# An attention and feed-forward kernel on one core: w_out loaded in four pieces, the fold in quarters, one part of q turned by a transfer, and all queues listed anew

## The chip, the core and the metric

The kernel runs on one core of a Trainium2 chip. A core has five engines that each follow their own queue of instructions: TensorE (PE, matmuls; its weight loads are listed as PEld), VectorE (DVE), ScalarE (ACT), GpSimd (POOL) and SyncE (SP, which only issues transfers here). 16 DMA engines move data; they are fed by POOL (loads that convert f32 to f16 on the way, and some others) and by SP (all other loads, the stores and the turning transfers). The metric is the device time of one execution in microseconds. A profiled execution gives a span, from its first to its last instruction, and there is some time around the span.

## The reference

Linear attention over 8 batches, 8 heads, 576 tokens and 64 channels per head, and then a gated product with four weight matrices, all in f32 at the boundary:

```python
q_s = softmax(q, axis=-1)          # over the 64 channels of a token
k_s = softmax(k, axis=2)           # over the 576 tokens of a batch
kv  = einsum('bhsd,bhse->bhde', k_s, v)
x   = einsum('bhsd,bhde->bhse', q_s, kv)     # -> 4608 x 512
a, b = x @ w1, x @ w2              # 512 -> 1024
h = a * b @ w3                     # 1024 -> 1024
out = h @ w_out                    # 1024 -> 512
```

Both softmaxes subtract a maximum first and add 1e-9 to the sum.

## The kernel before

Since nothing stands between w3 and w_out, the kernel first multiplies them: the **fold** W3O = w3 @ w_out, in eight row blocks ft of 128. After that each token costs two products with w1 and w2 and one with W3O.

All work is cut into named steps. A plan holds for each step its engine, what it needs and what buffers it takes. The class Plan emits the steps in the order of a written list, ORDER (lines 80 to 150), and each engine then runs its own steps in that order, one after another: a step that waits holds up all later steps of its engine. PICKS names the engine of the steps that can run on more than one. The tile framework puts in the waits for data. [...]

The names, for batch b (or chunk c, which is the first 512 tokens of the batch of the same number; chunk 8 is made of the last 64 tokens of every batch):

- loads: k.b, q.b, v.b, w1.i, w2.i (four column pieces each), w3.i (six row pieces) and wo.i (w_out). The first two parts of q go out on SP, the list LOADS on POOL, the rest on SP. A load on POOL waits for the landing of the one eight places ahead on POOL. q.0 and q.1 are loaded in two parts, q.b.0 (tokens blocks 0 to 3) and q.b.1 (blocks 4 to 8).
- fold: w3t.ft turns a block of w3 by eight TensorE transposes (line 415), w3T.ft moves it out of PSUM, pf.ft.h multiplies part h of it with part h of w_out (line 427), W3O.ft scales and stores the result (line 431). There are WOS parts, each of N_FT / WOS = 4 matmuls of 128x512 before the change.
- k: kmx (maximum), cb (the maximum brought to all partitions), ksub (subtract, line 490), kexp, and vc (v to f16, batches 2 and up). kv.b (lines 515 and 524) is the product with v, kv2.b divides by the sums.
- q: qmx, qsub (548), qexp (556), qsm (sum, 561), qeps, qrc (reciprocal), qn (multiply, 580), each in two parts p. Then q has to be turned so that channels lie on partitions. This is done in one of two ways: qt and qT are TensorE transposes (line 595) and an eviction from PSUM, qt.b.0 for part 0 and qt.b.8 and qt.b.16 for the blocks of part 1; or qd.b.p, one turning transfer on SP (line 603), for which DMAT[b][p] is set. Before the change batches 0 and 1 use TensorE and batches 2 to 7 the transfer.
- xm.b.h and xt.b (line 621) are the products with kv, for 512 tokens and for the last 64; xs and xts are their evictions.
- chunk: up.1 and up.0 (line 735) are the products with w2 and w1, bs evicts the first, ab (750) multiplies the two on DVE, down.c.tb (757) is the product with W3O, os its eviction and st.c.tb its store, as two transfers on SP.

Chunk 1 is worked in two halves of 256 tokens, so that xm.1.0 needs only part 0 of q of batch 1, and xm.1.1 and xt.1 need part 1.

PSUM is shared by rings: four buffers for up (and w3t), two for down and the fold, two for all of attention. The evicted outputs have four buffers in SBUF, so os waits for the store four places earlier. A load of batch b into a buffer of batch b - 2 waits for the exponentials of that batch (k.4 for kexp.2, q.4 for qexp.2).

FILL names two places where TensorE is given products of zeros: 17 at the start, and 16 ahead of pf.4.0.

Of the kernel before, what the change touches and what calls it, by code (L numbers as in the profile page):

```python
# [80 lines left out]
q.0.1 q.0.0 w3.4 k.0 wo.0 wo.1 ident w3.3 w3.0 qmx.0.1 w3.1 q.1.0 qsub.0.1 qexp.0.1 qmx.0.0 w3t.5
v.0 w3t.4 qsm.0.1 w3T.4 qsub.0.0 qeps.0.1 w3.5 qexp.0.0 kmx.0.0 w3T.5 w3.2 pf.4.0 qrc.0.1 cb.0
qn.0.1 pf.5.0 pf.4.1 qsm.0.0 k.1 qt.0.8 W3O.4 w2.0 w3t.3 qeps.0.0 ksub.0.1 pf.5.1 w3T.3 w1.0
qt.0.16 w3t.0 qrc.0.0 qT.0.8 qn.0.0 pf.3.0 kexp.0.1 pf.3.1 w3T.0 ksub.0.0 w3t.1 W3O.5 qt.0.0
w3T.1 W3O.3 pf.0.0 qmx.1.0 pf.1.0 kexp.0.0 qT.0.0 pf.0.1 qT.0.16 qsub.1.0 k.2 kv.0 w2.1 W3O.0
qexp.1.0 pf.1.1 w1.1 kv2.0 w3t.7 w2.2 qsm.1.0 w3t.6 w3T.7 xm.0.1 w1.2 w3t.2 xs.0.1.0 w3T.6 pf.7.0
W3O.1 xs.0.1.1 pf.7.1 qeps.1.0 pf.6.0 w3T.2 W3O.7 v.1 kmx.1.0 xm.0.0 pf.6.1 xs.0.0.1 xs.0.0.0
pf.2.0 w2.3 up.1.0.0.0 w1.3 qrc.1.0 up.0.0.0.0 cb.1 bs.0.0.0 qn.1.0 up.1.0.0.1 up.0.0.0.1
bs.0.0.1 ab.0.0.0 ksub.1.0 qt.1.0 kmx.2.0 pf.2.1 qT.1.0 up.1.0.0.2 W3O.2 xt.0 bs.0.0.2 q.1.1
ab.0.0.1 up.0.0.0.2 kexp.1.0 ksub.1.1 up.1.0.0.3 ab.0.0.2 xts.0.0 kmx.2.1 up.0.0.0.3 bs.0.0.3  # L90
up.1.0.0.4 up.0.0.0.4 bs.0.0.4 ab.0.0.3 kexp.1.1 up.1.0.0.5 xts.0.1 cb.2 up.0.0.0.5 W3O.6
bs.0.0.5 kv.1 q.2 ab.0.0.4 ksub.2.0 up.1.0.0.6 v.2 kv2.1 k.3 up.0.0.0.6 bs.0.0.6 ab.0.0.5 xm.1.0
ab.0.0.6 up.1.0.0.7 xs.1.0.1 ksub.2.1 xs.1.0.0 up.0.0.0.7 bs.0.0.7 qmx.1.1 kexp.2.0 up.1.1.0.0
up.0.1.0.0 ab.0.0.7 qsub.1.1 kexp.2.1 up.1.1.0.1 qmx.2.1 bs.1.0.0 up.0.1.0.1 bs.1.0.1 ab.1.0.0
down.0.0 qsub.2.1 qexp.1.1 qmx.2.0 vc.2.0 ab.1.0.1 q.3 up.1.1.0.2 v.3 qsm.1.1 vc.2.1 up.0.1.0.2
k.4 qexp.2.1 up.1.1.0.3 qsub.2.0 os.0.0 qsm.2.1 up.0.1.0.3 qeps.1.1 bs.1.0.2 kv.2 qrc.1.1
qexp.2.0 ab.1.0.2 down.0.1 qn.1.1 kv2.2 bs.1.0.3 q.4 st.0.0 ab.1.0.3 down.0.2 os.0.1 qmx.3.1
st.0.1 qt.1.8 os.0.2 qeps.2.1 qrc.2.1 qt.1.16 qsub.3.1 down.0.3 qsm.2.0 qT.1.8 st.0.2 qT.1.16
qmx.3.0 xm.1.1 down.1.0 xs.1.1.0 qn.2.1 kmx.3.1 xs.1.1.1 up.1.1.1.0 vc.3.0 qeps.2.0 up.0.1.1.0
qexp.3.1 qd.2.1 qrc.2.0 kmx.3.0 qn.2.0 xt.1 up.1.1.1.1 os.0.3 up.0.1.1.1 bs.1.1.0 xts.1.0  # L100
qsub.3.0 qd.2.0 up.1.1.1.2 xts.1.1 bs.1.1.1 qsm.3.1 ab.1.1.0 os.1.0 down.1.1 bs.1.1.2 ab.1.1.1
st.1.0 up.0.1.1.2 os.1.1 qmx.4.1 up.1.1.1.3 v.4 st.1.1 ab.1.1.2 up.0.1.1.3 bs.1.1.3 qeps.3.1
st.0.3 xm.2.0 vc.3.1 ab.1.1.3 down.1.2 xs.2.0.1 cb.3 xs.2.0.0 qsub.4.1 qexp.3.0 xm.2.1 down.1.3
xs.2.1.0 qrc.3.1 xs.2.1.1 qsm.3.0 ksub.3.1 qexp.4.1 up.1.2.0.0 up.0.2.0.0 qeps.3.0 bs.2.0.0
vc.4.0 qrc.3.0 up.1.2.0.1 ab.2.0.0 ksub.3.0 xt.2 kmx.4.0 bs.2.0.1 up.0.2.0.1 up.1.2.0.2
up.0.2.0.2 bs.2.0.2 qn.3.0 xts.2.1 ab.2.0.1 kexp.3.0 up.1.2.0.3 ab.2.0.2 up.0.2.0.3 qmx.4.0
bs.2.0.3 qn.3.1 kexp.3.1 up.1.2.0.4 os.1.2 up.0.2.0.4 bs.2.0.4 xts.2.0 ab.2.0.3 up.1.2.0.5 qd.3.1
qsm.4.1 qeps.4.1 up.0.2.0.5 bs.2.0.5 qd.3.0 kv.3 qrc.4.1 qsub.4.0 ab.2.0.4 up.1.2.0.6 k.5 kv2.3
up.0.2.0.6 q.5 bs.2.0.6 st.1.2 ab.2.0.5 qn.4.1 up.1.2.0.7 ab.2.0.6 up.0.2.0.7 bs.2.0.7 xm.3.1
ab.2.0.7 down.2.0 xs.3.1.1 qd.4.1 kmx.4.1 xs.3.1.0 os.1.3 v.5 xm.3.0 down.2.1 xs.3.0.1 cb.4  # L110
xs.3.0.0 os.2.0 up.1.3.0.0 st.2.0 xt.3 kmx.5.0 up.0.3.0.0 xts.3.1 ksub.4.0 st.1.3 bs.3.0.0
up.1.3.0.1 os.2.1 up.0.3.0.1 st.2.1 bs.3.0.1 qmx.5.0 xts.3.0 down.2.2 qexp.4.0 ksub.4.1 qmx.5.1
kexp.4.0 down.2.3 ab.3.0.0 qsub.5.1 ab.3.0.1 up.1.3.0.2 qsm.4.0 up.0.3.0.2 bs.3.0.2 qeps.4.0
qsub.5.0 up.1.3.0.3 kexp.4.1 ab.3.0.2 up.0.3.0.3 qrc.4.0 bs.3.0.3 up.1.3.0.4 qn.4.0 ab.3.0.3
qexp.5.0 os.2.2 up.0.3.0.4 bs.3.0.4 qsm.5.0 up.1.3.0.5 qexp.5.1 vc.4.1 qd.4.0 up.0.3.0.5 ab.3.0.4
bs.3.0.5 qsm.5.1 up.1.3.0.6 st.2.2 kv.4 bs.3.0.6 k.6 ab.3.0.5 up.0.3.0.6 qeps.5.0 q.6 qrc.5.0 v.6
qeps.5.1 up.1.3.0.7 kv2.4 qn.5.0 up.0.3.0.7 bs.3.0.7 ab.3.0.6 os.2.3 xm.4.1 ab.3.0.7 down.3.0
xs.4.1.1 qrc.5.1 xs.4.1.0 kmx.5.1 qn.5.1 xm.4.0 down.3.1 xs.4.0.1 xs.4.0.0 cb.5 qd.5.1 up.1.4.0.0
up.0.4.0.0 bs.4.0.0 os.3.0 up.1.4.0.1 ksub.5.1 ab.4.0.0 xt.4 qmx.6.1 bs.4.0.1 up.0.4.0.1 down.3.2
ksub.5.0 ab.4.0.1 kexp.5.1 up.1.4.0.2 vc.5.0 up.0.4.0.2 bs.4.0.2 vc.5.1 kexp.5.0 up.1.4.0.3  # L120
ab.4.0.2 qsub.6.1 up.0.4.0.3 xts.4.0 bs.4.0.3 k.7 os.3.2 qd.5.0 up.1.4.0.4 xts.4.1 ab.4.0.3 kv.5
bs.4.0.4 st.2.3 up.0.4.0.4 os.3.1 kv2.5 vc.6.0 st.3.0 up.1.4.0.5 ab.4.0.4 up.0.4.0.5 qexp.6.1
qmx.6.0 q.7 st.3.1 up.1.4.0.6 bs.4.0.5 qsub.6.0 up.0.4.0.6 v.7 bs.4.0.6 ab.4.0.5 st.3.2
up.1.4.0.7 ab.4.0.6 vc.6.1 qsm.6.1 xm.5.0 qexp.6.0 up.0.4.0.7 xs.5.0.0 down.3.3 qeps.6.1 bs.4.0.7
ab.4.0.7 qrc.6.1 xs.5.0.1 down.4.0 qsm.6.0 qn.6.1 os.3.3 st.3.3 kmx.6.0 xm.5.1 os.4.0 down.4.1
xs.5.1.0 st.4.0 xs.5.1.1 qeps.6.0 qrc.6.0 qd.6.1 xt.5 kmx.6.1 os.4.1 up.1.5.0.0 qn.6.0 xts.5.0
xts.5.1 up.0.5.0.0 st.4.1 vc.7.0 up.1.5.0.1 cb.6 qd.6.0 vc.7.1 up.0.5.0.1 down.4.2 bs.5.0.0
ksub.6.0 ab.5.0.0 up.1.5.0.2 os.4.2 bs.5.0.1 up.0.5.0.2 st.4.2 bs.5.0.2 ab.5.0.1 up.1.5.0.3
ab.5.0.2 ksub.6.1 kexp.6.0 bs.5.0.3 up.0.5.0.3 ab.5.0.3 up.1.5.0.4 qmx.7.1 up.0.5.0.4 bs.5.0.4
kexp.6.1 up.1.5.0.5 ab.5.0.4 qsub.7.1 up.0.5.0.5 bs.5.0.5 qmx.7.0 up.1.5.0.6 ab.5.0.5 kv.6  # L130
qsub.7.0 bs.5.0.6 qexp.7.1 up.0.5.0.6 kv2.6 up.1.5.0.7 ab.5.0.6 up.0.5.0.7 bs.5.0.7 qsm.7.1
# [744 lines left out]
```

## Time and profile before

| | us |
|---|---|
| median of 3 runs (243.4 to 244.03) | 243.53 |
| the profiled execution, its own time | 243.27 |
| its span | 241.5 |
| TensorE busy | 234.5 (97% of the span) |
| DVE busy | 170.8 |
| POOL busy | 124.0 |
| ACT busy | 123.4 |
| mean granted TensorE clock | 1.000 |
| moved by DMA | 45.66 MB, mean 189 GB/s |

The profile's page gives busy time per engine and the span in 40 slices. A timeline line gives the start, the length, the engine, the line of the kernel, the operation with output and inputs, and in brackets the idle time ahead of it with what ended it. The length of several matmuls in one line is from the start of the first to the modelled end of the last; the start of the next step is the better measure of when TensorE came free. The chain that ended last is followed back from the end of the span: 88% of it is TensorE.

### The profile page before, as it was taken

How to read it: one execution, taken by the hardware profiler on the slowest of the kernel's cores; microseconds unless marked ns; L12 is line 12 of the kernel's file. 1: busy time of each engine (PE TensorE's matmuls, PEld its weight loads, DVE VectorE, ACT ScalarE, POOL GpSimd, SP SyncE). 2: the span in 40 equal slices, each digit the busy share in tenths (PEclk: the TensorE clock that was granted, in tenths of full speed). 3: DMA queues.
4: the chain of work that ended last, by engine and by line, in shares of the span. 5: the costliest groups of instructions: out<-in, count | busy, mean ns of one | idle time of the engine just before them, and what ended most of it. 6: DMA issues, size and time to landing. Idle time of an engine off the chain costs nothing.

```text
span 241.5 us, 4827 instructions
## 1 busy us (share of the span) xinstructions
PE 234.5 (97%) x1917; PEld 114.6 (47%) x1917; DVE 170.8 (71%) x293; ACT 123.4 (51%) x194; POOL 124.0 (51%) x79
## 2 busy tenths in 40 slices
PE   7889999999999999999999999999999999999994
...
PEclk9999999999999999999999999999999999999999
DMA  6999999999999808992897999701750215000343
GB/s 209 310 209 250 305 302 200 249 370 356 399 388 160 274 1 114 380 341 83 206 400 124 248 401 281 153 0 35 165 76 3 49 38 133 0 0 0 88 132 130
DMA packets 37894, 45.66 MB, mean 189 GB/s; under 512 B 15984, under 2 KB 22384, under 8 KB 37872
## 3 DMA queue, kind: packets, MB, share of 16 engines
...
q14 instruction: 7, 0.06, 0.1%
...
## 4 chain that ended last, share of the span: by engine, by line
PE 88%; DMA 7%; POOL 2%; issue 1%; ACT 0%; POOLq 0%
PE pab L735 52%; PE po L757 23%; DMA v<-in_v_dram 7%; PE po L772 3%; PE po L427 3%; PE pkv L515 2%; PE xm L621 2%; POOL w L377 1%; PE w3t L415 1%; PE xt L621 1%; PE pkv L524 1%; POOL wosb L377 0%; PE qtp L595 0%; POOL q L377 0%; POOL k L377 0%
## 5 line engine op out<-in xcount | busy, mean ns | idle before, releaser
L750 DVE TENSOR_TENSOR ab<-pab,bsb 128x512 f16<-128x512 f32 x72 | 48.8, 684 | 28.4 <-PE pab L735 24.8
L735 PE MATMUL pab<-x,w1sb 128*128 128x512 f16 (+1 forms) x288 | 65.9, 356 | 0.0
L735 PE MATMUL pab<-x,w2sb 128*128 128x512 f16 (+1 forms) x288 | 65.8, 356 | 0.0
L298 ACT CAST bsb<-pab 128x512 f16<-128x512 f32 x59 | 34.6, 586 | 52.0 <-PE pab L735 51.7
L757 PE MATMUL po<-W3O,ab 128*128 128x512 f16 x256 | 59.5, 380 | 0.0
L490 POOL TENSOR_TENSOR k<-k,cb 128x1152 f32<-128x1152 f32 x15 | 39.2, 2629 | 20.3 <-DVE cb L486 19.1
L735 PEld LDWEIGHTS <-w2sb 128*128 128x128 f16 x320 | 30.7, 98 | 30.6 <-issue 0.2
L735 PEld LDWEIGHTS <-w1sb 128*128 128x128 f16 x320 | 30.6, 98 | 29.6 <-issue 0.2
L580 POOL TENSOR_TENSOR en<-eq,qr 128x1280 f16<-128x1280 f16 (+1 forms) x15 | 32.1, 2141 | 15.3 <-ACT x L302 6.3
L757 PEld LDWEIGHTS <-ab 128*128 128x128 f16 x256 | 24.0, 98 | 29.2 <-issue 2.7
L548 POOL TENSOR_TENSOR q<-q,qm 128x1024 f32<-128x1024 f32 (+1 forms) x14 | 29.7, 2126 | 8.6 <-DVE qm L543 6.3
L298 ACT COPY osb<-po 128x512 f32<-128x512 f32 (+1 forms) x29 | 16.6, 572 | 28.5 <-PE po L757 22.6
L459 DVE TENSOR_REDUCE km<-k 128x128 f32<-128x1152 f32 x12 | 25.4, 2115 | 0.0
L543 DVE TENSOR_REDUCE qm<-q 128x20 f32<-128x1280 f32 (+1 forms) x16 | 21.4, 1344 | 4.1 <-DMA q<-in_q_dram 4.1
L302 ACT ACTIVATE x<-xm 128x512 f16<-128x512 f32 x30 | 16.5, 595 | 10.0 <-PE xm L621 9.8
L561 DVE TENSOR_REDUCE qr<-eq 128x20 f32<-128x1280 f16 (+1 forms) x16 | 21.3, 1330 | 0.4 <-ACT eq L556 0.4
L556 ACT ACTIVATE eq<-q 128x1280 f16<-128x1280 f32 (+1 forms) x16 | 18.6, 1165 | 5.6 <-POOL q L548 2.9
L498 ACT ACTIVATE ek<-k 128x1152 f16<-128x1152 f32 x16 | 18.5, 1164 | 2.5 <-POOL k L490 2.5
L298 DVE CAST bsb<-pab 128x512 f16<-128x512 f32 x13 | 9.0, 690 | 13.4 <-PE pab L735 13.3
L427 PE MATMUL po<-wosb,w3T 128*128 128x512 f16 x64 | 15.3, 379 | 1.2 <-DMA wosb<-in_moe_w_out_dram 1.2
L325 PE MATMUL po<-zero 128*128 128x512 f16 x33 | 10.0, 470 | 1.6 <-DVE zero L320 1.6
L427 PEld LDWEIGHTS <-w3T 128*128 128x128 f16 x64 | 5.8, 98 | 7.8 <-ACT w3T L298 1.2
...
## 6 DMA issues: line engine op xcount, KB each, us to landing
...
```

Source lines behind the costliest of these rows:

```text
L298: return [(nc.scalar.copy if eng == "ACT" else engine[eng].tensor_copy)(out=out, in_=in_)]
L427: nc.tensor.matmul(st["pf", ft], lhsT=st["w3T", ft][:, gt, :], rhs=wosb[:, gt, :], start=(gt == 0), stop=(gt == N_FT - 1))
L459: dve.tensor_reduce(out=st["km", b][:, two(hp), :], in_=kb[:, two(hp), :, :].rearrange("p h j d -> p h d j"), axis=AX.X, op=ALU.max)
L490: return [engine[eng].tensor_tensor(out=kb[:, two(hp), :, :], in0=kb[:, two(hp), :, :], in1=st["cb", b][:, two(hp), None, :].broadcast_to( ...
L543: dve.tensor_reduce(out=st["qm", b][:, :, j], in_=qb[:, :, j, :], axis=AX.X, op=ALU.max)
L548: return [engine[eng].tensor_tensor(out=qb[:, :, j, :], in0=qb[:, :, j, :], in1=st["qm", b][:, :, j, None].broadcast_to([P, HH, n, D]), op ...
L556: nc.scalar.activation(out=st["eq", b, p], in_=qb[:, :, j, :], func=AF.Exp)
L561: dve.tensor_reduce(out=st["qr", b][:, :, slice(*PARTS[p])], in_=st["eq", b, p], axis=AX.X, op=ALU.add)
L580: return [engine[eng].tensor_tensor(out=st["en", b][:, j, :, :].rearrange("p j h d -> p h j d"), in0=st["eq", b, p], in1=st["qr", b][:, :, ...
L735: nc.tensor.matmul(st["p", one, c, sub, u][:, a * (t1 - t0):(a + 1) * (t1 - t0)], lhsT=w[:, ct, fb * P:(fb + 1) * P], rhs=x()[:, ct, t0:t1 ...
L750: dve.tensor_tensor(out=st["ab", c][:, nf * u:nf * u + nf, t0:t1], in0=cut(st["p", 0, c, sub, u]), in1=cut(st["bsb", c, sub, u]), op=ALU.mult)
L757: nc.tensor.matmul(st["po", c, tb], lhsT=st["ab", c][:, ft, tb * P:(tb + 1) * P], rhs=W3O[:, ft, :], start=(ft == 0), stop=(ft == N_FT - 1))
```

## The change

1. WOS goes from 2 to 4: w_out is loaded in four pieces of 256 KB (as f16), in the order 0, 2, 1, 3, and each pf step has two matmuls.
2. DMATP = [(1, 1)]: part 1 of q of batch 1 is turned by the transfer qd.1.1 on SP. The steps qt.1.8, qt.1.16, qT.1.8 and qT.1.16 go.
3. ORDER, LOADS, PICKS, FILL and LINKED are new. In the list the differences reach to about batch 5. FILL now has 12 zero products ahead of qt.0.8 and none ahead of pf.4.0.

Core of the diff, with the loads and with the parts of the list that the prediction speaks of:

```diff
-LINKED = 191
+LINKED = 212
 FILL = {
-    "begin": 17, "pf.4.0": 16,
+    "begin": 17, "qt.0.8": 12,
 }
 LOADS = [
-    ("w3", 4), ("k", 0), ("wo", 0), ("wo", 1), ("w3", 3), ("w3", 0), ("w3", 1), ("q", 1, 0),
-    ("v", 0), ("w3", 5), ("w3", 2), ("k", 1), ("w2", 0), ("w1", 0), ("k", 2), ("w2", 1),
-    ("w1", 1), ("w2", 2), ("w1", 2), ("v", 1), ("w2", 3), ("w1", 3), ("q", 1, 1),
+    ("w3", 4), ("k", 0), ("wo", 0), ("wo", 2), ("wo", 1), ("wo", 3), ("w3", 3), ("w3", 0),
+    ("w3", 1), ("q", 1, 0), ("w3", 5), ("v", 0), ("w3", 2), ("k", 1), ("w1", 0), ("w2", 0),
+    ("k", 2), ("w2", 1), ("w1", 1), ("w2", 2), ("w1", 2), ("v", 1), ("w2", 3), ("w1", 3),
+    ("q", 1, 1),
 ]
-    WOS = 2
+    WOS = 4
-    DMATP = []
+    DMATP = [(1, 1)]
     DMAT = [[b > DMATS or (b, p) in DMATP for p in range(2)] for b in range(B)]
```

The list, sorted by engine (TensorE to the first up, POOL to the end of the loads, SP from its third load to the transposes of batch 2):

```
PE before:  w3t.5 w3t.4 pf.4.0 pf.5.0 pf.4.1 qt.0.8 w3t.3 pf.5.1 qt.0.16 w3t.0 pf.3.0 pf.3.1 w3t.1
            qt.0.0 pf.0.0 pf.1.0 pf.0.1 kv.0 pf.1.1 w3t.7 w3t.6 xm.0.1 w3t.2 pf.7.0 pf.7.1 pf.6.0
            xm.0.0 pf.6.1 pf.2.0 up.1.0.0.0
PE after:   w3t.5 w3t.4 qt.0.8 pf.4.0 pf.5.0 pf.5.1 pf.4.1 pf.4.2 pf.4.3 w3t.3 pf.5.2 pf.5.3 w3t.0
            pf.3.0 pf.3.1 pf.3.2 qt.0.0 w3t.1 pf.0.0 qt.0.16 pf.0.1 pf.3.3 pf.0.2 pf.0.3 pf.1.0 pf.1.1
            w3t.7 pf.1.2 pf.1.3 w3t.6 kv.0 pf.7.0 pf.7.1 pf.7.2 pf.7.3 xm.0.1 w3t.2 pf.6.0 pf.6.1
            pf.6.2 xm.0.0 pf.6.3 pf.2.0 pf.2.1 pf.2.2 up.1.0.0.0
POOL before: w3.4 k.0 wo.0 wo.1 ident w3.3 w3.0 w3.1 q.1.0 v.0 qsub.0.0 w3.5 w3.2 qn.0.1 k.1 w2.0 w1.0
            ksub.0.0 k.2 w2.1 w1.1 w2.2 w1.2 v.1 w2.3 w1.3 qn.1.0 ksub.1.0 q.1.1 ksub.1.1
POOL after: w3.4 k.0 wo.0 wo.2 wo.1 wo.3 w3.3 w3.0 ident w3.1 qsub.0.0 q.1.0 w3.5 v.0 w3.2 qn.0.0
            ksub.0.0 k.1 w1.0 w2.0 k.2 w2.1 w1.1 w2.2 w1.2 v.1 w2.3 qn.1.0 ksub.1.1 ksub.1.0 w1.3 q.1.1
SP before:  q.2 v.2 k.3 q.3 v.3 k.4 q.4 st.0.0 st.0.1 st.0.2 qd.2.1 qd.2.0 st.1.0
SP after:   q.2 v.2 k.3 q.3 v.3 qd.1.1 st.0.0 k.4 q.4 qd.2.1 qd.2.0 st.0.1 st.0.2 v.4 st.1.0
```

Further on: down.1.0 comes ahead of xm.1.1 (before: behind it); on POOL qn.1.1 comes ahead of qsub.2.0 and vc.3.1 behind ksub.3; on ACT qexp.2.0 comes behind os.0.2; for chunks 3 and up bs.c.0.5 moves from ACT to DVE and the first os of a chunk from DVE to ACT.

More of the change, by code (lines that the diff above doesn't have):

```diff
@@ L75, in run @@
                 held = s["eng"], got[-1]
-LINKED = 191
+LINKED = 212
 ORDER = """
[L81 to L131, printed above, removed]
+q.0.1 q.0.0 w3.4 k.0 wo.0 wo.2 wo.1 wo.3 w3.3 qmx.0.1 w3.0 ident qsub.0.1 qexp.0.1 qmx.0.0 w3.1
+w3t.5 w3t.4 qsm.0.1 qsub.0.0 qeps.0.1 w3T.4 qrc.0.1 q.1.0 qn.0.1 w3T.5 w3.5 kmx.0.0 qexp.0.0
@@ new lines @@
+qt.0.8 pf.4.0 v.0 pf.5.0 qT.0.8 w3.2 pf.5.1 pf.4.1 qsm.0.0 pf.4.2 pf.4.3 qeps.0.0 W3O.4 qrc.0.0
+cb.0 qn.0.0 w3t.3 pf.5.2 w3T.3 pf.5.3 w3t.0 W3O.5 pf.3.0 ksub.0.1 w3T.0 pf.3.1 pf.3.2 qt.0.0
+ksub.0.0 kexp.0.1 w3t.1 qmx.1.0 pf.0.0 qt.0.16 pf.0.1 pf.3.3 qT.0.16 pf.0.2 W3O.3 w3T.1 pf.0.3
+k.1 kexp.0.0 qsub.1.0 pf.1.0 w1.0 pf.1.1 w3t.7 w2.0 qT.0.0 qexp.1.0 pf.1.2 W3O.0 pf.1.3 k.2 w3t.6
+w3T.7 qsm.1.0 w2.1 kv.0 w3T.6 w1.1 w2.2 qeps.1.0 pf.7.0 kv2.0 pf.7.1 w1.2 pf.7.2 W3O.1 pf.7.3
+xm.0.1 W3O.7 w3t.2 xs.0.1.1 xs.0.1.0 pf.6.0 qrc.1.0 v.1 pf.6.1 w3T.2 kmx.1.0 pf.6.2 xm.0.0 pf.6.3
@@ new lines @@
+up.1.1.0.0 bs.0.0.7 W3O.6 up.0.1.0.0 ab.0.0.7 qsub.1.1 bs.1.0.0 qmx.2.1 up.1.1.0.1 up.0.1.0.1
+bs.1.0.1 ab.1.0.0 qsub.2.1 down.0.0 qexp.1.1 ab.1.0.1 qmx.2.0 q.3 up.1.1.0.2 os.0.0 v.3 qsm.1.1
+vc.2.1 up.0.1.0.2 bs.1.0.2 up.1.1.0.3 ab.1.0.2 qeps.1.1 qexp.2.1 down.0.1 qrc.1.1 kmx.3.0 qn.1.1
+kexp.2.1 down.0.2 vc.2.0 qsm.2.1 qsub.2.0 qd.1.1 os.0.1 up.0.1.0.3 qmx.3.1 bs.1.0.3 ab.1.0.3
+st.0.0 kv.2 os.0.2 down.0.3 qexp.2.0 kv2.2 k.4 qsub.3.1 q.4 down.1.0 os.0.3 qsm.2.0 qeps.2.1
+qeps.2.0 qrc.2.1 xm.1.1 qmx.3.0 qn.2.1 down.1.1 xs.1.1.0 xs.1.1.1 qrc.2.0 kmx.3.1 qexp.3.1
```

38 lines of the change are left out of this document (added), and 36 rows, old and new, of the table PICKS.

## The prediction

> **What bounds the kernel now.** I read the page first (engines, slices), then the chain that ended last in order of time, then TensorE's own timeline step by step, and last the DMA issues, one at a time, for the time from issue to landing. The page:
>
> ```profile
> span 241.5 us, 4827 instructions
> PE 234.5 (97%) x1917; PEld 114.6 (47%) x1917; DVE 170.8 (71%) x293; ACT 123.4 (51%) x194; POOL 124.0 (51%) x79
> PE   7889999999999999999999999999999999999994
> PEclk9999999999999999999999999999999999999999
> DMA  6999999999999808992897999701750215000343
> ```
>
> TensorE (PE) is the bound, at full granted clock. The 16 DMA engines are full until about 73 us, with holes later. In TensorE's timeline, starts of neighbouring steps can be subtracted: a 128x512 matmul takes 0.216 us, and from 16.5 us to 238.2 us there is almost no gap. The waits that remain are at the start:
>
> ```profile
> 14.14 1.89 PE L427 MATMUL po<-wosb,w3T 128*128 128x512 f16 x8 [0.75 <-DMA wosb<-in_moe_w_out_dram]
> 16.48 1.02 PE L427 MATMUL po<-wosb,w3T 128*128 128x512 f16 x4 [0.45 <-DMA wosb<-in_moe_w_out_dram]
> 25.32 0.48 PE L515 MATMUL pkv<-v,ek 64*64 64x64 f16 x36 [0.16 <-DMA v<-in_v_dram]
> 27.72 0.46 PE L415 MATMUL w3t<-ident,w 128*128 128x128 f16 x4
> ```
>
> The reader should see that the fold (L427) waits for w_out, and kv.0 (L515) for v of batch 0. So early TensorE runs at the pace of landings. Those, by issue plus time to landing: w_out 14.0 and 16.4; w3.3 17.7; w3.0 18.9; w3.1 20.3; q.1.0 21.7; v.0 25.2; w3.5 27.7; w3.2 28.9. In the chain, the piece that the change takes out and the product that follows the next transfers:
>
> ```profile
> 8.97 16.22 DMA v<-in_v_dram
> ...
> 65.06 0.56 PE qtp L595 x10
> ...
> 78.52 0.34 PE xm L621 x4
> ```
>
> And the queue that will carry the new transfer, with POOL's normalisations (L580) that feed it:
>
> ```profile
> 61.09 2.34 POOL L580 TENSOR_TENSOR en<-eq,qr 128x1280 f16<-128x1280 f16 x1 [0.31 <-DVE qr L573]
> 61.90 0.37 SPq L377 DMA_DIRECT2D q<-in_q_dram  x1
> 62.32 4.50 SPq L783 DMA_DIRECT2D out_dram<-osb  x6
> 69.48 5.22 SPq L603 DMA_TRANSPOSE qT<-en  x2
> ```
>
> The six stores (st.0.0 to st.0.2) go ahead of the two transposes of batch 2, which land at 77.2 and 77.4 (7.7 and 5.3 us after issue). xm.2.0, which needs both, starts at 78.45: 1.05 us to spare.
>
> **The change part by part.** Steps are named as in the order list (section on the kernel).
>
> *Turn of q.1.1 off TensorE.* Ten transposes less: 0.56 us (row above), all on the path, since TensorE has no gap there: **-0.56**. ACT loses two evictions (1.29 us together), off the path.
>
> *w_out in quarters, fold in quarters, less filler.* Two more loads on POOL, 0.55 us each (two took 1.09): ident moves from about 4.6 to 6.8 us, covered, because w3.4 lands at 8.65. Bytes are the same, and 256 KB pieces land 1.2 to 1.4 us apart (w3.3, w3.0, w3.1) against 2.45 for 512 KB, so a pair costs between -0.05 and +0.35 against one; I take 0. The quarters should land at about 12.8, 14.0, 15.2 and 16.4. qn.0.1 now runs on DVE (1.22 us x 20/16 = 1.5) right after its sum, and qt.0.8 can run at about 13.1 instead of 17.34. But w3t.3 and w3t.0 still wait for w3.3 and w3.0 (17.7, 18.9): at 19.25 both kernels stand at w3t.0 with the same fold work done. So this gain is spent before it counts: 0. The filler (16 before pf.4.0, 3.62 us; now 12 before qt.0.8, some 2.7) lies inside these waits: 0; without them it would cost its 2.7.
>
> *The load list.* w3.5 is now ahead of v.0 (both behind q.1.0). Same bytes, so w3.5 lands at about 24.9 and v.0 in w3.5's old place, 27.7. TensorE's list from w3t.0 at 19.25 to kv.0 is four w3t (4 x 0.49), twelve quarters of the fold (24 matmuls x 0.216 = 5.17) and qt.0.0 and qt.0.16 (0.45 + 0.11), 7.7 us in all: it stands at kv.0 at 26.95 and waits 0.75. From kv.0's start the old kernel had 241.5 - 25.32 = 216.18 us to go; pf.1.1, w3t.7 and w3t.6 (26.76 to 28.86 = 2.10) are now done earlier. End: 27.7 + 216.18 - 2.10 = 241.78, that is **+0.28**. Bounds: v.0 by 26.95 gives -0.47; a late v.0 (two pair surcharges of 0.35) gives +0.98. I take the middle row, 27.7, a landing of the same bytes.
>
> *Other queues up to 60 us.* qn.0.0 moves to POOL (1.91), ksub.0.0 ends near 23.5, before v.0, and k.1, w1.0 and w2.0 are issued behind it instead of ahead: the DMA engines still hold w3.5, v.0 and w3.2 until 28.9, so nothing starves. w2.0 now lands after w1.0, at 34.6; up.1.0.0.0 stands at 35.4. w1.3 moves behind ksub.1.0 on POOL (issue near 42.8 instead of 34.86), still before w2.3's landing at 46.95, so it keeps 48.25 against a need at 49.4. If that 1.1 us of cover goes, it costs what is lacking. [...]
>
> *The new transfer.* q.1.1's sums end near 60.5, qn.1.1 near 62.9 (63.4 before; qsub.2.0, 1.91, now waits behind it). qd.1.1 then sits on SP behind v.3, whose bytes land at 65.9. A single transpose behind a load landed 1.0 to 1.9 us after that load (batch 4's after q.5, batch 5's two after v.6 and k.7), so it lands at 66.9 to 67.8. xm.1.1 moves behind down.1.0: 67.27 - 0.56 + 1.73 + 0.28 = 68.7. In time by about 1 us: 0.
>
> *What is queued behind it.* On SP st.0.0, k.4 and q.4 wait behind qd.1.1, and st.0.1, st.0.2 now behind qd.2.0. Before, k.4 was issued at 57.5 and q.4 at 61.9; now k.4 at 65.3 to 67.3 and q.4 after qexp.2.0 (moved on ACT to near 66.6). q.4 landed at 72.6. With k.5 and q.5, issued into an empty queue at 94.06 and 94.89, landing took 6.3 and 8.6 us, so q.4 now lands at 74.2 to 76.4, mid 75.3. The pair qd.2.1, qd.2.0 landed 4.0 us after what stood ahead (stores, near 73.3). qn.2.0 also ends later, near 73.1 instead of 72.3, which alone gives 73.2 + 5.3 = 78.5. xm.2.0 stands at 78.45 + 0.28 - 0.56 = 78.2. Wait: 0.3 from qn's side, 75.3 + 4.0 - 78.2 = 1.1 from the queue's. Bounds: 0 and 76.4 + 4.0 - 78.2 = 2.2. I take 1.1, since it is from the same pair behind the same load: **+1.1**. st.0.1's later landing (near 78.5) is needed by os.1.1 near 80: 0.
>
> [...]
>
> *From 80 us on.* os.c.0 goes to ACT and bs.c.0.5 to DVE for c of 3 and up: as many on each as before. xs of the second half of x then ends 0.4 us ahead of xt. vc.3.1 now runs after ksub.3 on POOL, so qd.3.0 lands near 97.0 against xm.3.1 at 97.5. Both 0, with little to spare.
>
> **Sum:** +0.28 - 0.56 + 1.1 = +0.82 us on the span, 242.3. The profiled execution took 243.27 (span 241.5 and 1.77 around it), 0.26 below the median of the runs, 243.53. On the median: **244.3**. About 0.3% (0.73 us) is what a measurement of this kernel can tell from no change: 242.8 and 244.26 are the marks.
>
> **The rivals.**
> - *No wait at xm.2.0* (the end on the other side): k.4 goes out early enough and the pair lands before 78.2; what decides is q.4's landing, before or after 74.2. For it: SP took only 1.24 to 1.39 us for a transpose in a quiet queue, and four stores (some 1.3 us of traffic) leave the stretch. Against: 1.05 us was all there was. Then -0.28, 243.25; with v.0 by 26.95, -1.03, 242.5. Chance 0.36, 0.22 of it below 242.8.
> - *qd.1.1 itself is late.* A transpose behind loads took up to 8.6 us from issue (batch 4): 62.9 + 8.6 = 71.5, xm.1.1 waits 2.8, and the later wait vanishes in it: +2.5, 246.0; partly so, 245. It decides from a landing after 68.7. Against it: v.3 lands at 65.9. Chance 0.14.
> - *The change does nothing that counts:* the early list is bound by landings, the transfers fit, v.0 a little late takes back the 0.56: 243.5. Chance 0.06.
> - *Pieces in series.* If each extra w_out piece cost a whole store's time (256 KB, 2.0 us), all later landings move by 4.0: 248. The w3 pieces, 1.2 to 1.4 apart, speak against it. Chance 0.02. [...]
>
> **How the numbers follow.** The forecast case, a wait at xm.2.0 of 0.7 to 1.8 us (243.95 to 245.0), has 0.42; 0.12 of it lies below 244.26. Faster: 0.22. Same: 0.12 + 0.14 + 0.06 = 0.32. Slower: 0.30 + 0.14 + 0.02 = 0.46. Range 242.5 to 245.4: from the first rival's end to part of the second's, leaving out some 0.05 below and 0.12 above. The forecast case's own range is 243.95 to 245.0.
>
> **What would show it.** Right: kv.0's pkv waits some 0.7 us for v; the first pf steps are before 15 us but w3t.0 still starts near 19; qtp x10 is gone from 65 us; xm of batch 1 starts without a wait near 68.7; xm of batch 2 is the one place in mid-kernel where TensorE waits, for DMA qT. Wrong: kv.0 without a wait (start gains 0.75), no gap before xm of batch 2 (the first rival), a gap before xm of batch 1 (the second), or a wait where a relisted queue holds TensorE at a place that I priced at nothing: up.0.0.0.6 (w1.3), xm.3.1, or an xt.

## The result, and the profile after

The changed kernel takes 244.63 us (median of 244.49 to 245.06, four runs) against 243.54 for the kernel before in the same comparison: a ratio of 1.0046, with a 95% interval of 1.0029 to 1.0064. It is slower by about 1.1 us, more than the 0.73 us that the prediction took as the least that can be told from no change. Run again later, as it is, it took 244.89 (six runs; ratio 1.0054, 1.0034 to 1.0074). The forecast was 244.3.

The profiled execution is the slowest of the first four (245.06, span 243.3; the spans of the others are 242.6 to 243.0). Its page:

```profile
span 243.3 us, 4796 instructions
PE 232.8 (96%) x1903; PEld 113.4 (47%) x1903; DVE 172.5 (71%) x291; ACT 122.4 (50%) x194; POOL 124.4 (51%) x81
PE   7669999999999899999999999999999999999994
PEclk9999999999999999999999999999999999999999
DMA  6999999999999946994948999600740115000334
```

TensorE is busy 1.7 us less than before and the span is 1.8 us longer, so it waits more. One of the new waits shows as an 8 in the fourteenth slice of its row (79 to 85 us), the others in the first three, where the changed kernel also has four zero products fewer. TensorE's timeline at the start (columns as before: start, length, engine, line, operation, and in brackets the idle time with what ended it; line numbers are 2 higher than before):

```profile
13.95 1.03 PE L429 MATMUL po<-wosb,w3T 128*128 128x512 f16 x4
15.67 1.90 PE L429 MATMUL po<-wosb,w3T 128*128 128x512 f16 x8 [0.70 <-DMA wosb<-in_moe_w_out_dram]
18.22 0.71 PE L417 MATMUL w3t<-ident,w 128*128 128x128 f16 x8 [0.65 <-DMA w<-in_moe_w_dram]
28.03 0.48 PE L517 MATMUL pkv<-v,ek 64*64 64x64 f16 x36 [0.19 <-DMA v<-in_v_dram]
```

The fold now starts before 14 us, and the time won is then spent waiting for the third piece of w_out and for w3.3. w3t.0 starts at 19.64, and kv.0 at 28.03 where it was at 25.32, with 2.10 us of fold work done earlier in exchange. Then SP's queue, and the chain of waits:

```profile
63.19 1.72 SPq L605 DMA_TRANSPOSE qT<-en  x1
66.29 0.53 SPq L379 DMA_DIRECT2D k<-in_k_dram  x1
66.92 1.24 SPq L379 DMA_DIRECT2D q<-in_q_dram  x1
71.15 5.67 SPq L605 DMA_TRANSPOSE qT<-en  x2
```

```profile
14.67 13.23 DMA v<-in_v_dram
...
73.78 6.41 DMA qT<-en
80.24 0.41 PE xm L623 x4
```

The transfer of q.1.1 holds k.4 back on SP, to 66.3, and q.4 goes behind it at 66.9. With the transfer undone (below) they go at 62.7 and 66.3: there q.4 goes when qexp.2.0, which the new list has later, has freed its buffer. So the transfer delays q.4 itself by 0.6 only, but it puts all of k.4 right ahead of it. Taken one at a time, the issues of SP show q.4 landing 9.9 us after its issue, at 76.8, and the pair qd.2.1 and qd.2.0 behind it at 79.4 and 80.2. xm.2.0, ready at 78.5, starts at 80.24: a gap of 1.74, of which the profile gives 1.56 to the transfer. The chain runs through this transfer now, where it ran from matmul to matmul.

The profile of the second comparison differs in one place:

```profile
69.76 0.41 PE L623 MATMUL xm<-qT,kv 64*64 64x256 f16 x8 [0.58 <-DMA qT<-en]
80.48 0.41 PE L623 MATMUL xm<-qT,kv 64*64 64x512 f16 x4 [1.19 <-DMA qT<-en]
```

There q.3 landed 1.1 later, v.3 landed at 67.0 (the first profile has no record of its landing), and qd.1.1 landed at 69.6, not 67.1, so xm.1.1 waits too, in a gap of 0.75, and xm.2.0 less, in one of 1.37.

### The profile page after: what moved, and what is told of

Its sections match the earlier page's. It is cut to its first block, busy times and chain, and to the rows that moved or that the text cites. A ratio compares the mean times of both kernels' runs of the same rounds, so it can differ in the third digit from the quotient of the medians.

```text
span 243.3 us, 4796 instructions
## 1 busy us (share of the span) xinstructions
PE 232.8 (96%) x1903; PEld 113.4 (47%) x1903; DVE 172.5 (71%) x291; ACT 122.4 (50%) x194; POOL 124.4 (51%) x81
## 4 chain that ended last, share of the span: by engine, by line
PE 82%; DMA 13%; POOL 2%; issue 1%; ACT 0%; DVE 0%; POOLq 0%; ACTq 0%
PE pab L737 49%; PE po L759 22%; DMA v<-in_v_dram 5%; DMA wosb<-in_moe_w_out_dram 5%; PE po L774 3%; DMA qT<-en 3%; PE pkv L517 2%; PE po L429 2%; PE xm L623 2%; POOL en L582 1%; PE xt L623 1%; PE pkv L526 1%; ACT osb L300 0%; POOL w L379 0%; POOL q L550 0%
## 5 line engine op out<-in xcount | busy, mean ns | idle before, releaser
L300 ACT CAST bsb<-pab 128x512 f16<-128x512 f32 x50 | 29.4, 587 | 45.7 <-PE pab L737 42.9
L582 POOL TENSOR_TENSOR en<-eq,qr 128x1024 f16<-128x1024 f16 (+1 forms) x15 | 31.5, 2108 | 21.2 <-DVE qr L575 10.8
L300 ACT COPY osb<-po 128x512 f32<-128x512 f32 (+1 forms) x35 | 20.3, 579 | 34.5 <-PE po L759 29.2
L300 DVE CAST bsb<-pab 128x512 f16<-128x512 f32 x22 | 15.1, 688 | 14.8 <-PE pab L737 14.3
L429 PE MATMUL po<-wosb,w3T 128*128 128x512 f16 x64 | 15.8, 380 | 0.7 <-DMA wosb<-in_moe_w_out_dram 0.7
L327 PE MATMUL po<-zero 128*128 128x512 f16 x29 | 8.3, 451 | 1.6 <-DVE zero L322 1.6
```

What stands on the lines that cost most here:

```text
L300: return [(nc.scalar.copy if eng == "ACT" else engine[eng].tensor_copy)(out=out, in_=in_)]
L429: nc.tensor.matmul(st["pf", ft], lhsT=st["w3T", ft][:, gt, :], rhs=wosb[:, gt, :], start=(gt == 0), stop=(gt == N_FT - 1))
L582: return [engine[eng].tensor_tensor(out=st["en", b][:, j, :, :].rearrange("p j h d -> p h j d"), in0=st["eq", b, p], in1=st["qr", b][:, :, ...
```

## The experiments

Theory: the start costs a few tenths, since v.0 is listed behind w3.5, and the rest is the wait at xm.2.0, caused by the loads that now stand ahead of the pair on SP. Rivals: four pieces of w_out are dear by themselves; or the new transfer has a cost of its own. Each experiment is compared with runs of the kernel before on the same chip; their medians are 243.47 to 243.51.

### k.4 behind the pair

```diff
-SP: v.3 qd.1.1 st.0.0 k.4 q.4 qd.2.1 qd.2.0 st.0.1 st.0.2
+SP: v.3 qd.1.1 st.0.0 q.4 qd.2.1 qd.2.0 k.4 st.0.1 st.0.2
-    "bs_2_0_1": "DVE"
+    "bs_2_0_1": "ACT"
```

(From the changed kernel; kmx.4.0, which reads k.4, comes behind ab.2.0.0 on DVE to suit.)

> The changed kernel, but on SP k.4 goes behind qd.2.0 and q.4 is the one load ahead of the pair qd.2.1, qd.2.0; kmx.4.0 moves on DVE behind ab.2.0.0, and bs.2.0.1 to ACT, so that DVE does not wait for the late k.4. Theory (the pair waits for the loads ahead of it in the queue): one load of 1152 KB less ahead of the pair, some 3 us, so the pair lands by 77.5 to 78.5, xm.2.0 (78.5) waits 0 to 0.3 instead of 1.74, and the time falls by 1.4 to 1.7 us against the changed kernel, to 243.0 to 243.3. Rival (the pair is late because qn.2.0 and SP's own handling are late, not for the load): the pair still lands near 80, no change, 244.6.

Measured: 246.00, ratio 1.0093 (1.0069 to 1.0118). ACT and TensorE in its timeline:

```profile
78.61 0.41 PE L621 MATMUL xm<-qT,kv 64*64 64x512 f16 x4
82.76 0.59 ACT L298 COPY osb<-po 128x512 f32<-128x512 f32 x1 [2.60 <-DMA out_dram<-osb]
83.40 0.81 PE L757 MATMUL po<-W3O,ab 128*128 128x512 f16 x3 [1.73 <-ACT osb L298]
```

The wait at xm.2.0 is gone, so the loads ahead were its cause. But the kernel is slower still: the osb buffers are four in a ring, so os.1.1 needs st.0.1 landed, and st.0.1, still behind the pair, now stood behind k.4 as well (it landed at 82.4 and 82.7). A wait of 1.74 was exchanged for one of 1.80 (and two of 0.47 and 0.29 at other places). I had not priced the store.

### The transfer undone

```diff
-    DMATP = [(1, 1)]
+    DMATP = []
-PE: down.0.3 down.1.0 xm.1.1
+PE: down.0.3 qt.1.8 qt.1.16 down.1.0 xm.1.1
```

> The changed kernel with one part undone: part 1 of q of batch 1 is turned on TensorE again (qt.1.8 and qt.1.16 ahead of down.1.0, their evictions on ACT behind qeps.2.1); the start in quarters and the order of the loads stay. Theory: TensorE has 0.56 us more, st.0.0 and k.4 are no longer held on SP, the pair lands near 77.5, and xm.2.0 (near 79.1) does not wait: 244.6 + 0.56 - 1.74 = 243.4 to 243.6, that is the time before, with only the start's surplus left. Rival (the start and the new list make the loss, the transfer gains its 0.56): 245.2.

Measured: 244.72, ratio 1.0047 (1.0032 to 1.0061). No wait at xm.2.0, as expected, but no gain in time. Besides the start, the profile has one new wait. PE, POOL and DVE in its timeline:

```profile
78.24 2.34 POOL L548 TENSOR_TENSOR q<-q,qm 128x1280 f32<-128x1280 f32 x1 [3.13 <-DVE qm L543]
...
78.68 1.93 DVE L569 TENSOR_SCALAR qr<-qr 128x20 f32<-128x20 f32 x1
80.53 0.68 DVE L750 TENSOR_TENSOR ab<-pab,bsb 128x512 f16<-128x512 f32 x1
...
81.26 0.61 PE L757 MATMUL po<-W3O,ab 128*128 128x512 f16 x2 [0.30 <-DVE ab L750]
```

qeps.3.1 (L569) adds a constant to 128x20 numbers. It takes 1.93 here, beside POOL's subtraction, and ends 0.03 after it; and ab.1.1.3 behind it comes late for down.1.2: a gap of 0.46. The same 1.93 is in the changed kernel, at 78.90, hidden behind the wait at xm.2.0. So that wait had a second, smaller one under it.

### The transfer alone, on the list of before

```diff
-    DMATP = []
+    DMATP = [(1, 1)]
-SP: v.3 k.4 q.4 st.0.0 st.0.1 st.0.2 qd.2.1 qd.2.0
+SP: v.3 qd.1.1 k.4 q.4 st.0.0 st.0.1 st.0.2 qd.2.1 qd.2.0
-PE: qt.1.8 qt.1.16 down.0.3 xm.1.1 down.1.0 up.1.1.1.0
+PE: down.0.3 down.1.0 xm.1.1 up.1.1.1.0
```

> The kernel before with one part alone: qd.1.1 instead of the four TensorE and ACT steps, on SP between v.3 and k.4, xm.1.1 behind down.1.0; loads, fold, stores and picks as before. Theory: SP holds k.4 and q.4 until qn.1.1 is done at 63.4, the six stores still go ahead of the pair, so the pair lands 3 to 4 us later than its 77.4, near 81; xm.2.0, now at 77.9, waits some 3 us: 243.5 - 0.56 + 3 = 246. Rival (the pair has 1.05 us to spare and the queue catches up): at most 0.5 us of wait, 243.0 to 243.5.

Measured: 245.66, ratio 1.0091 (1.0065 to 1.0117), on the start of before. TensorE's timeline:

```profile
69.56 0.27 PE L733 MATMUL pab<-x,w2sb 128*128 128x256 f16 x1 [0.68 <-ACT x L300]
70.05 0.92 PE L733 MATMUL pab<-x,w2sb 128*128 128x256 f16 x7 [0.22 <-ACT x L300]
...
80.80 0.41 PE L619 MATMUL xm<-qT,kv 64*64 64x512 f16 x4 [1.70 <-DMA qT<-en]
```

The wait at xm.2.0 (a gap of 1.87) comes with the transfer and needs neither the quarters nor the new list. The 0.75 and 0.38 at up.1.1.1.0 are my edit's: with down.1.0 ahead of xm.1.1, nothing was left to cover the evictions of x.

### v.0 ahead of w3.5

```diff
-    ("q", 1, 0), ("w3", 5), ("v", 0), ("w3", 2)
+    ("q", 1, 0), ("v", 0), ("w3", 5), ("w3", 2)
-PE: pf.1.0 pf.1.1 w3t.7 pf.1.2 pf.1.3 w3t.6 kv.0 pf.7.0
+PE: pf.1.0 pf.1.1 kv.0 pf.1.2 pf.1.3 w3t.7 w3t.6 xm.0.1 w3t.2 pf.7.0
-DVE: qsub.1.0 qT.0.0
+DVE: qT.0.0 qsub.1.0
```

> The changed kernel with v.0 loaded ahead of w3.5 again, kv.0 ahead of pf.1.2, and xm.0.1 and w3t.2 ahead of pf.7, qT.0.0 ahead of qsub.1.0 on DVE. Theory (the early list runs at the pace of landings): kv.0 starts near 25.8 instead of 28.0, w3t.7 waits for w3.5 near 28, and by 30.1 as much is done as now at 30.5: 0.3 to 0.4 us faster than the changed kernel, but xm.2.0 then waits that much longer, since the pair does not move, so the time changes by 0 to -0.2: 244.4 to 244.6. Rival (the whole gain at the start comes through): 244.2.

Measured: 244.82, ratio 1.0044 (1.0026 to 1.0062). TensorE's timeline:

```profile
25.71 0.48 PE L515 MATMUL pkv<-v,ek 64*64 64x64 f16 x36 [0.19 <-DMA v<-in_v_dram]
...
69.59 0.41 PE L621 MATMUL xm<-qT,kv 64*64 64x256 f16 x8 [0.52 <-DMA qT<-en]
79.65 0.41 PE L621 MATMUL xm<-qT,kv 64*64 64x512 f16 x4 [0.54 <-DMA qT<-en]
```

kv.0 is 2.3 us earlier and the time is that of the changed kernel. With gaps of 0.69 and 0.71 the transfers take back what the start may have gained. The place of v.0, which my sum named as the cost of the start, is at most a small part of it (accounting below).

### The quarters alone, twice

On the list of before: four loads and four pf steps in the places of two, nothing else.

```diff
-    WOS = 2
+    WOS = 4
-POOL: wo.0 wo.1 ident w3.3 w3.0 w3.1 q.1.0 v.0 qsub.0.0 w3.5 w3.2 qn.0.1
+POOL: wo.0 wo.1 wo.2 wo.3 ident w3.3 w3.0 w3.1 q.1.0 v.0 qsub.0.0 w3.5 w3.2 qn.0.1
```

> The quarters alone, on the list of before: w_out in four pieces and pf in quarters, each pair of pieces in the place of the half it replaces, the transposes kept on TensorE. Theory (the start is bound by the landings of the list of loads, and more pieces put those behind them later; the kernel changed landed v.0 at 27.87 where the list alone would have given 27.7, w3.3 at 18.22 against 17.7): v.0 is ahead of w3.5 here, so kv.0 starts at 25.5 to 25.7 against 25.28 in before, and the time is 243.6 to 244.0. Rival (the quarters let fold work start earlier and fill the start): kv.0 before 25.2 and the time 243.0 to 243.3.

Measured: 247.04, ratio 1.0161 (1.0135 to 1.0188), far outside both. POOL, ACT and TensorE in its timeline, and the clock row of its page:

```profile
12.03 0.77 POOL L376 DMA_DIRECT2D q<-in_q_dram  x1 [2.45 <-DMA k<-in_k_dram]
13.92 1.92 POOL L547 TENSOR_TENSOR q<-q,qm 128x1024 f32<-128x1024 f32 x1
15.87 1.06 ACT L555 ACTIVATE eq<-q 128x1024 f16<-128x1024 f32 x1 [4.59 <-POOL q L547]
17.88 2.64 PE L426 MATMUL po<-wosb,w3T 128*128 128x512 f16 x8 [3.15 <-ACT w3T L297]
23.09 1.91 PE L426 MATMUL po<-wosb,w3T 128*128 128x512 f16 x4
```

```profile
PEclk9995999999999999999999999999999999999999
```

The loads on POOL after the eighth (at 9.05, 12.03 and 13.15 here) each go out when the one eight places ahead has landed. Two more loads in the list make q.1.0 the tenth instead of the eighth, so its issue moves from 6.1 to 12.0, and qsub.0.0, listed behind it, begins at 13.92 where it began at 9.74. ACT waits for that with w3T.5 behind it, and TensorE stands for 3.31. Then the granted clock is halved for a time (the 5 in the fourth slice; 0.50 from 20 to 24 us): four matmuls of 128x512 take 1.91 at 23.09 (1.03 at 18.77 in the changed kernel). At 20 us TensorE stands for about 1.1 more, at half clock already (the 1.52 in the next expectation counts its last matmul there at the full clock). This profile is of the slowest of the six executions, 248.98; one that kept its full clock took 246.94, so most of the loss is the stand and not the clock.

So the second kernel moves those loads behind the computations, on POOL alone:

```diff
-POOL: w3.3 w3.0 w3.1 q.1.0 v.0 qsub.0.0 w3.5 w3.2 qn.0.1 k.1
+POOL: w3.3 w3.0 w3.1 qsub.0.0 q.1.0 v.0 qn.0.1 w3.5 w3.2 k.1
```

> Quarters alone on the list of before once more, with POOL's list mended: q.1.0 and v.0 behind qsub.0.0, w3.5 and w3.2 behind qn.0.1 (all POOL). In the run of quarters alone POOL's ninth and tenth transfers were issued at 9.0 and 12.0, each just after the landing of the one eight places ahead, and qsub.0.0, listed behind them, began at 12 or later where it had begun at about 9, so that ACT waited 4.59 for it and TensorE 3.31 and 1.52. Theory (four pieces take four of the eight places, and what was listed behind the ninth and tenth transfer waits): with the two computations ahead, no gap over 1.0 before 25 us, no halved clock, kv.0 at 25.3 to 26, and 243.5 to 244.3. Rival (quarters cost the start by themselves, in whatever order): 245.5 or more.

Measured: 243.49, ratio 0.9999 (0.9990 to 1.0007): the time of the kernel before. TensorE's timeline:

```profile
14.15 1.89 PE L426 MATMUL po<-wosb,w3T 128*128 128x512 f16 x8 [0.26 <-DMA wosb<-in_moe_w_out_dram]
16.72 0.59 PE L426 MATMUL po<-wosb,w3T 128*128 128x512 f16 x2 [0.68 <-DMA wosb<-in_moe_w_out_dram]
25.33 0.48 PE L514 MATMUL pkv<-v,ek 64*64 64x64 f16 x36
```

The fold starts 0.8 us earlier, at 13.30, and kv.0 at the same time as before (25.32). Here pieces half as large neither gained nor cost, once POOL's list was fitted to them.

### ab.1.1.3 ahead of the small addition

From the kernel with the transfer undone:

```diff
-DVE: ab.1.1.2 qeps.3.1 ab.1.1.3
+DVE: ab.1.1.2 ab.1.1.3 qeps.3.1
```

> The kernel changed with the transfer of q of batch 1 undone (the ten transposes back on TensorE), and ab.1.1.3 moved ahead of qeps.3.1 on DVE. Theory (the 0.46 wait of down.1.2's last matmuls in that run came from qeps.3.1, an addition of 128x20 that took 1.93 while POOL's subtraction ran beside it, and stood ahead of ab.1.1.3): no wait of TensorE between 79 and 81, and a time 0.4 below that kernel's 244.72, 244.2 to 244.4. Rival (ab.1.1.3 is late for its own operands): the wait stays, 244.6 to 244.8.

Measured: 244.15, ratio 1.0029 (1.0019 to 1.0038), 0.57 below the kernel without this edit (0.68 above before in its own comparison, against 1.21 there). DVE in its timeline:

```profile
79.42 0.69 DVE L750 TENSOR_TENSOR ab<-pab,bsb 128x512 f16<-128x512 f32 x1 [0.57 <-PE pab L735]
80.03 0.68 DVE L569 TENSOR_SCALAR qr<-qr 128x20 f32<-128x20 f32 x1
```

TensorE has no gap over 0.25 between 30 and 230 us left here, and there is no transfer of q.1.1. Yet the time is 0.68 above before. That is what the new list costs without the transfer, and the accounting below puts it at the start.

### The changed kernel mended

```diff
-SP: qd.1.1 st.0.0 k.4 q.4 qd.2.1 qd.2.0 st.0.1 st.0.2
+SP: qd.1.1 st.0.0 q.4 st.0.1 st.0.2 qd.2.1 qd.2.0 k.4
-DVE: xm.2.0 qeps.3.1 ab.1.1.3
+DVE: xm.2.0 ab.1.1.3 qeps.3.1
```

(kmx.4.0 comes later and bs.2.0.1 goes to ACT, as in the run with k.4 behind the pair.)

> The kernel changed with three moves on queues: k.4 behind the pair qd.2.1 and qd.2.0 on SP, st.0.1 and st.0.2 ahead of the pair (they stood behind it), ab.1.1.3 ahead of qeps.3.1 on DVE; kmx.4.0 stands later to suit. Theory (the wait at xm.2.0 is k.4's and q.4's bytes ahead of the pair, the wait of os.1.1 is a store behind k.4, the small one is qeps.3.1): no wait over 0.3 between 68 and 83, what is left is the start, and the time is 243.3 to 243.8. Rival (the stores ahead hold the pair as the loads did): xm.2.0 still waits 0.5 to 1.5 on the pair, 244.0 to 244.8.

Measured: 244.29 (243.53 to 245.05, twelve runs), ratio 1.0031 (1.0019 to 1.0043). In TensorE's timeline xm.2.0 does not wait:

```profile
78.43 0.41 PE L621 MATMUL xm<-qT,kv 64*64 64x512 f16 x4
```

The profiled execution is the fastest, 243.53, inside the range of the theory; the median is not. The pair landed at 77.8, 0.6 ahead of xm.2.0. The others may have been later there or at xm.1.1, but they left no trace, so this is not shown.

### The transfer on the list of before, with every mend

```diff
-SP: v.3 k.4 q.4 st.0.0 st.0.1 st.0.2 qd.2.1 qd.2.0 st.1.0
+SP: v.3 qd.1.1 st.0.0 q.4 st.0.1 st.0.2 qd.2.1 qd.2.0 k.4 st.1.0
-PE: qt.1.8 qt.1.16 down.0.3 xm.1.1 down.1.0 up.1.1.1.0
+PE: down.0.3 down.1.0 xm.1.1 down.1.1 up.1.1.1.0
-DVE: qeps.3.1 ab.1.1.3
+DVE: ab.1.1.3 qeps.3.1
```

(k.4's reader kmx.4.0 stays where it is; os.0.3 comes ahead of xm.1.1 on ACT, which frees the PSUM buffer of down.1.1.)

> The list of before (halves of w_out, v.0 ahead of w3.5) with the transfer of q of batch 1 and all that the runs asked for around it: k.4 behind the pair on SP, st.0.0 and st.0.1 not behind loads, down.1.1 between xm.1.1 and up.1.1.1.0 with os.0.3 ahead of it, ab.1.1.3 ahead of qeps.3.1. Theory (the transfer is worth its 0.56 of TensorE where nothing near it waits): no wait over 0.3 between 66 and 83, kv.0 at 25.3, the time 242.9 to 243.2, below both kernels. Rival (some wait always comes with the transfer): 243.5 or more, with a named wait in that stretch.

Measured: 244.22, ratio 1.0031 (1.0017 to 1.0045): the rival. One gap of 1.40 in the middle of TensorE's timeline:

```profile
79.33 0.41 PE L619 MATMUL xm<-qT,kv 64*64 64x512 f16 x4 [1.23 <-DMA qT<-en]
```

On this list qn.1.1 ends a microsecond later, so qd.1.1 went out at 64.1 and q.4 at 67.8 (66.1 in the mended kernel above, where it landed at 72.7). Here q.4 landed at 74.4 and the pair at 78.4 and 79.3. One load ahead is enough, when it goes out late.

### q.4, too, behind the pair

On both mended kernels; qmx.4.1, qsub.4.1 and qexp.4.1 (and qsm.4.1 in the second) come later to suit.

```diff
-SP: q.4 st.0.1 st.0.2 qd.2.1 qd.2.0 k.4
+SP: st.0.1 st.0.2 qd.2.1 qd.2.0 q.4 k.4
```

On the list of before:

> The transfer on the list of before, with the moves of the last such run, and q.4 too behind the pair on SP (qmx.4.1, qsub.4.1 and qexp.4.1 later to suit). There the pair, behind q.4 alone (landed 74.4), landed at 78.4 and 79.25 and xm.2.0 waited 1.4. Theory (a transpose behind a load lands some us after that load, whichever it is, and the transfer is worth its 0.56 where nothing waits): the pair lands by 76.5, no gap over 0.3 between 66 and 84, and the time is 242.8 to 243.2, below before. Rival (the pair's own time, two transposes in a row, is what is late): the pair lands at 78 or later and xm.2.0 waits 0.5 to 1.5, 243.6 or more.

On the changed list:

> The kernel changed with the moves of its mended run (k.4 behind the pair, st.0.1 and st.0.2 ahead of it, ab.1.1.3 ahead of qeps.3.1), and q.4 too behind the pair. Theory (in the mended run the pair came 0.4 before xm.2.0 in the profile, and in its slower executions later than that): with margin the times draw together at the profiled value, 243.4 to 243.7, which is before's time less 0.56 for the transposes and plus 0.5 to 0.6 for the start. Rival (the spread comes from the start): the median stays at 244.1 to 244.4 with a range of over 1 us.

Measured: 246.03 (1.0098, 1.0067 to 1.0129) and 248.05 (1.0191, 1.0167 to 1.0216). The issues of the first from 69 to 80 us (last column: median us to landing), then TensorE and ACT in its timeline:

```profile
v<-in_v_dram SPq DMA_DIRECT2D x1, 1152.0 KB, 10.6
qT<-en SPq DMA_TRANSPOSE x2, 3.5
```

```profile
77.93 0.41 PE L619 MATMUL xm<-qT,kv 64*64 64x512 f16 x4
88.69 1.16 ACT L296 CAST v<-v 128x1152 f16<-128x1152 f32 x1 [6.04 <-DMA v<-in_v_dram]
90.37 1.02 PE L733 MATMUL pab<-x,w2sb 128*128 128x512 f16 x4 [2.55 <-ACT bsb L296]
```

and of the second from 71 to 80 us:

```profile
qT<-en SPq DMA_TRANSPOSE x2, 3.3
```

With no load ahead a transpose of the pair lands 3.2 to 3.5 us after its issue in both kernels (the pair by 77.1 and 76.3), and xm.2.0 does not wait. In the first of them qd.2.0 went out at 73.56, only 0.2 earlier than in the changed kernel (73.78), and landed 3.1 earlier: so it was not qn.2.0 or SP that made it late there, but the loads ahead. But now q.4, k.4 and v.4 stand one behind another. In the first kernel v.4 lands at 88.7, ACT's cast of it waits 6.04, bs steps stand behind the cast, and TensorE waits 2.72 for those. In the second kernel ACT and DVE, in their new order, hold TensorE for 1.83 and two gaps of 0.4, qd.3 is late in its turn (1.72), and xm.1.1 waits 0.46 for qd.1.1.

### The changed kernel again

> The kernel changed, as it is, for a second profile and more times. If the 1.74 gap ahead of xm.2.0 in its first profile (245.06, the slowest of its four runs) is the usual one, the median is near 245 and the gap again 1.6 to 1.9; if the other three runs (244.49 to 244.73) are the usual ones, the median is 244.5 to 244.7 and the gap 1.0 to 1.5, by what those runs are shorter than the profiled one. The start up to kv.0 should be as before within 0.2: kv.0 at 27.8 to 28.1.

Measured: 244.89, with the two gaps shown at the top, and kv.0 at 27.99 as expected. Neither reading is quite right: the median lies between, and in this profile a gap at xm.1.1 takes part of the place of the one at xm.2.0.

### The accounting

From each profile: the span less before's 241.5, plus 0.56 where the ten transposes are off TensorE; of that, the gaps of TensorE from 65 to 95 us; and the remainder, which is the start and all else.

| kernel | span | lost | gaps 65 to 95 | remainder |
|---|---|---|---|---|
| transfer alone, list of before | 243.8 | 2.86 | 3.00 | -0.14 |
| the same, mended | 242.4 | 1.46 | 1.40 | 0.06 |
| quarters alone, mended | 241.5 | 0 | 0 | 0 |
| changed | 243.3 | 2.36 | 1.74 | 0.62 |
| changed, again | 243.5 | 2.56 | 2.12 | 0.44 |
| k.4 late | 244.2 | 3.26 | 2.56 | 0.70 |
| v.0 first | 242.7 | 1.76 | 1.40 | 0.36 |
| transfer undone | 242.7 | 1.20 | 0.46 | 0.74 |
| the same, ab.1.1.3 first | 242.4 | 0.90 | 0 | 0.90 |
| changed, mended | 241.8 | 0.86 | 0.29 | 0.57 |

With the start of before the remainder is zero within 0.14, so by this accounting the transposes are worth their 0.56. On the changed list it is 0.36 to 0.90, whatever is done at 70 us. The two kernels with q.4 behind the pair fit as well: on the changed list 5.36 is lost, 4.82 of it in gaps up to 103 us, which leaves 0.54; on the list of before 4.46, of which 2.72 is the gap and 1.7 the 3.4 us at half clock that follow it (last section).

That the remainder lies in the start can be read directly, at the first product with w2, up.1.0.0.0. Before, and in the changed kernel:

```profile
34.51 1.03 PE L735 MATMUL pab<-x,w2sb 128*128 128x512 f16 x4
```

```profile
35.66 1.03 PE L737 MATMUL pab<-x,w2sb 128*128 128x512 f16 x4
```

The eight profiles on the changed list have it at 35.48 to 35.73; those of the transfer on the list of before (three kernels) and of the quarters alone, mended, at 34.50 to 34.55. Two matmuls of the fold, 0.43, are done ahead of it on the changed list and behind it before; the other 0.5 to 0.8 is the cost of the new start. With v.0 first it is at 35.51, no earlier than the others.

## Why the prediction was right, point by point

*The outcome.* Slower by about 0.45%, with the largest wait where it was put. The forecast case's own range (243.95 to 245.0) holds both medians.

*Turn of q.1.1 off TensorE, -0.56.* Right: qtp x10 is gone from 65 us, and the accounting closes with that value. No run shows it as time gained.

*Quarters, 0.* Right, by the second kernel with quarters alone (0.9999). The gain of the early fold was spent waiting, as said: pf from 13.95, w3t.0 at 19.64 against a forecast of 19.25. The cost that quarters do have I passed over: they use up places among the loads in flight on POOL, eight here (the ninth and tenth went out at 9.05 and 12.03, behind the landings of the first and second). The changed list had already moved its computations to suit, and only the first of the two experiments shows the price (3.6 us, the halved clock in some executions included).

*The load list, +0.28.* This term was too small, and its reason was not the right one. By its own arithmetic kv.0 at 28.03 instead of 27.7 makes it +0.61; without the transfer and without waits the time was +0.68, and by the first product with w2 the start costs 0.5 to 0.8. TensorE stood at kv.0 later than I had it (27.7, not 26.95), so the wait for v there is 0.34, not 0.75. Putting v.0 first moved kv.0 by 2.3 us and left a remainder of 0.36 still. Which part of the new start costs it (order of the pieces and of the fold, qn.0.1 on DVE, filler ahead of qt.0.8) was not separated.

*The new transfer in time, 0.* Right in the first profile (landed 67.1, forecast 66.9 to 67.8; xm.1.1 at 69.16 without a wait), wrong in the second (69.6, a gap of 0.75), and wrong with v.0 first (0.69) and with q.4 behind the pair on the changed list (0.46). The rival of a late qd.1.1 is therefore not another world but part of some executions, with a size of 0.5 to 0.75 rather than 2.5.

*What is queued behind it, +1.1.* Mechanism right, and shown three ways: the wait comes with the transfer alone, goes with k.4 moved, and stays away with no load ahead. Its size in the profiles was 1.74 and 1.37. Two terms behind that size were off, in opposite directions. q.4 landed at 76.8, 1.5 later than my middle value, since its landing took 9.9 us against the 8.6 of the row I used; the pair then came 3.4 us behind it, not 4.0. The 4.0 was a misreading of the kernel before, and so were the 1.05 us to spare. The second transpose of its pair went out at 72.61 and took 5.4 us:

```profile
72.61 2.08 SPq L603 DMA_TRANSPOSE qT<-en  x1
```

```profile
qT<-en SPq DMA_TRANSPOSE x1, 5.4
```

So it landed at 78.0, not 77.4: xm.2.0 had 0.45 us to spare, and the pair was complete 3.5 us behind the last store ahead of it (74.5). With 3.5 the sum's own wait is 0.6. By the medians (1.09 and 1.41 above before), with 0.6 at the start and the 0.56, all waits together are 1.05 and 1.37; that the forecast 1.1 comes so near is partly luck. From its issue a transpose of the pair took 3.2 to 3.5 us with no load ahead, and 8.2 and 6.4 behind the loads of the changed kernel.

*st.0.1 for os.1.1, 0.* Right here only because xm.2.0 waits first; with that wait gone it was 1.80. qeps.3.1, worth 0.46 in the same way, I had not seen. No wait showed at up.0.0.0.6, xm.3.1 or an xt.

*LINKED, 191 to 212.* For the first LINKED names of the list, link (line 839 of the kernel before) makes a step of DVE or POOL that is marked in the plan wait for the marked step ahead of it, where that is on the other of the two. No run took the 21 more names alone.
